# The small-part product of a split fp32r matrix product, taken in bf16

## The chip, the cores and the metric

The kernel runs on one core of one Trainium2 chip. The metric is the device time of one execution in microseconds (us); a run's value is the median of several executions. The core has TensorE (PE in the profile, with its weight loads as PEld), VectorE (DVE), ScalarE (ACT), GpSimd (POOL) and SyncE (SP, which here only issues DMAs). They run side by side and wait for one another through semaphores.

## The reference, cut to what matters

```python
# x (8, 4096, 192), weight_gen (8, 4096, 8, 7), w_in (192, 2048), w_out (2048, 192); all float32 values
w = softmax(weight_gen, axis=-1)                # 7 taps for each row and head
x_unf = the 7 last rows of x, padded with zeros # (B, S, 7, 8 heads, 24)
x = einsum('bshk,bskhg->bshg', w, x_unf).reshape(32768, 192)

h = x @ w_in                                    # the first product, 192 -> 2048
g = h * np.cos(h)
out = g @ w_out                                 # the second product, 2048 -> 192
```

So each row of x is mixed with the six rows before it, the result goes through a product with 2048 columns, each element h becomes h cos h, and a second product brings 2048 back to 192. `w_in` and `w_out` come as float64 words, which the kernel takes apart itself.

## The kernel before, in words

**Batches and periods.** The 32768 rows are worked off in 64 batches of 512 rows (`NB`, 4 rows on each of 128 partitions). The 2048 columns between the two products are taken 256 at a time, as a pair of 128-column chunks, so that a batch has 8 pairs. One pass of the main loop (line 604) handles one pair of one batch; it is called a period below. There are 512 of them, and a few more to drain.

**Split operands.** Both products are made of parts. A value v is cut in v_hi, its fp32r rounding, and v_lo, the rest. The first product is x_lo·w_hi + x_hi·w_lo + x_hi·w_hi, all in fp32r (`ffn_in_first` and `ffn_in_second`, lines 333 to 361). In the second product g_hi meets both parts of `w_out` in one matmul of 384 columns in fp32r, and g_lo, written as bf16, meets a bf16 copy of `w_out` (`wo_b`) in one of 192 columns (`ffn_out`, line 403). So PE already changes between fp32r and bf16 within each period.

**Pairs of matmuls.** The contraction over 192 is cut in three pieces of 64. A matmul of 64 rows uses half of the array; the code issues them two by two, `q` = 0 on partitions 0 to 63 and `q` = 1 on partitions 64 to 127, and the two run side by side. Below, a "pair" of matmuls is such a couple. `wa_hi` and `wa_lo` hold the pieces that meet their own 64 rows of x directly, `wb_hi` and `wb_lo` (half as wide) the middle piece of each chunk. In a period `ffn_in_first` has 3 pairs of 512 columns (line 342) and `ffn_in_second` 6 (line 359); 3 of these 9 have x_lo as the moving operand. `ffn_out` has 8 pairs of 384 and 8 pairs of 192 columns (line 427).

**The order on PE in a period i**: `ffn_in_first(i)`, then `ffn_out(i-6)`: its fp32r half, one pair of small transposes of a later batch's x (line 321), its bf16 half; then `ffn_in_second(i)`. Two periods of every 32 split the bf16 half of `ffn_out` in two and put `ffn_in_first` between them (line 639). All engines work in the order in which the code issues; line 708 onwards pins it.

**The other engines in a period.** ACT turns h into whole turns (line 369), takes the sine (line 383), rounds g to fp32r (line 393), copies the second product's sum out of PSUM every second period (line 450), and rounds the transposed x to x_hi (line 301). DVE takes the fraction (line 379), multiplies (line 386), and writes g_lo as bf16 (line 397). POOL mixes the rows of x with the taps (lines 261 and 276), adds up the outputs (lines 466 and 467), and writes x_lo = x - x_hi (line 303) one 256-column piece at a time. In four batches of the start DVE writes x_lo whole. Once in 32 periods there is a round of softmax for the next 16 rows: ACT loads the table of the exponential, applies it to the taps (line 209) and loads the table of the sine again; in that period DVE makes the turns instead (line 375), and POOL has the sums and scalings of the taps (lines 185 to 188, 217, 206 and 226).

**PSUM.** The tiles `h` take three buffers of two banks, in turn; the sum of the second product (`acc`) takes the last two banks. A period's `h` may be written when DVE is done with the `h` of three periods ago, and `acc` again when ACT has copied it.

**The weights** are cut by `two_parts` (line 124) in steps spread over the first eight periods: ACT makes the size word (134), DVE the bits (136, 140, 144), ACT the fp32r part (147) and, where a `half` is given, a bf16 copy of the whole value (149), POOL the rest (150). Only `w_out` is given a `half` before the change.

The main loop's order around the products, of which the prediction speaks:

```python
if i < N:
    ffn_in_first(i, h_now if whole is None else whole)
if j >= 0:
    ffn_out(j)
...
if i < N:
    ffn_in_second(i)
...
if j >= 0:
    evacuate(j)
```

Of the kernel before, what the change touches and what calls it, by code (L numbers as in the profile page):

```python
# [12 lines left out]
F32R = mybir.dt.float32r  # L13
I32 = mybir.dt.int32
U16 = mybir.dt.uint16
BF16 = mybir.dt.bfloat16
# [4 lines left out]
P = 128  # L21
# [22 lines left out]
def tile_softmax_conv_then_cos_ffn(  # L44
# [14 lines left out]
    F = w_in.shape[1]  # L59
# [4 lines left out]
    CT = R * P  # L64
# [12 lines left out]
    const = ctx.enter_context(tc.tile_pool(name="const", bufs=1))  # L77
    gpool = ctx.enter_context(tc.tile_pool(name="gpool", bufs=9))
    work = ctx.enter_context(tc.tile_pool(name="work", bufs=2))
# [3 lines left out]
    def h_banks(k):  # L83

        return ps_h.tile([P, 2, CT], F32, name="h", tag=f"h{k % 3}", bufs=1)
# [12 lines left out]

    wa_hi = const.tile([P, F], F32R, name="wa_hi")
    wa_lo = const.tile([P, F], F32R, name="wa_lo")  # L100

    wb_hi = const.tile([P, F // 2], F32R, name="wb_hi")
    wb_lo = const.tile([P, F // 2], F32R, name="wb_lo")
    wo = const.tile([P, NFC, 2 * D], F32R, name="wo")
    wo_b = const.tile([P, NFC, D], BF16, name="wo_b")

    def words(n, home="ghi"):

        if home == "ghi":
            raw = gpool.tile([P, 2 * CW], I32, name="raw", tag=home)  # L110
        elif home == "fin":
            raw = work.tile([P, R * D], I32, name="raw", tag=home)
        else:
            raw = work.tile([P, 2 * CT], I32, name="raw", tag=home)
        return raw[:, 0:2 * n]
# [8 lines left out]
    def two_parts(raw, hi, lo, half=None):  # L124
        shape = hi.shape[1:]
        n = math.prod(shape)

        def shaped(t, steps):
            t = t.rearrange("p (n s) -> p n s", s=steps)
            return t if len(shape) == 1 else t.rearrange("p (a b) s -> p a b s", b=shape[1])  # L130

        low, top = (shaped(raw, 2)[..., k] for k in range(2))
        size, bits = (shaped(t[:, 0:n], 1)[..., 0] for t in room.pop(0))
        nc.scalar.activation(out=size.bitcast(F32), in_=top.bitcast(F32), func=AF.Abs, scale=F64_SCALE)
        yield
        nc.vector.tensor_scalar(  # L136
            out=size, in0=size, scalar1=3, scalar2=None, op0=ALU.logical_shift_left)
        yield

        nc.vector.scalar_tensor_tensor(  # L140
            out=size, in0=top, scalar=-0x80000000, in1=size, op0=ALU.bitwise_and, op1=ALU.bitwise_or)
        yield

        nc.vector.scalar_tensor_tensor(  # L144
            out=bits, in0=low, scalar=29, in1=size, op0=ALU.logical_shift_right, op1=ALU.bitwise_or)
        yield
        nc.scalar.copy(out=hi, in_=bits.bitcast(F32))
        if half is not None:
            nc.scalar.copy(out=half, in_=bits.bitcast(F32))
        nc.gpsimd.tensor_tensor(out=lo, in0=bits.bitcast(F32), in1=hi.bitcast(F32), op=ALU.subtract)  # L150

    def w_in_a(c0, c1, home="ghi"):
        raw = words(c1 - c0, home)
        for n in range(2):
            nc.sync.dma_start(out=raw[n * D2:(n + 1) * D2],
                              in_=w_in[n * P:n * P + D2, c0:c1].bitcast(I32))
        return two_parts(raw, wa_hi[:, c0:c1], wa_lo[:, c0:c1])

    w_in_odd_even = w_in.rearrange("k (a n c) -> n k a c", n=2, c=P)

    def w_in_b(j):
        raw = words(CW)
        pairs = slice(j * CW // P, (j + 1) * CW // P)
        for n in range(2):
            nc.sync.dma_start(out=raw[n * D2:(n + 1) * D2].rearrange("k (a c) -> k a c", c=2 * P),
                              in_=w_in_odd_even[1 - n, D2:P, pairs, :].bitcast(I32))
        cols = slice(j * CW, (j + 1) * CW)
        return two_parts(raw, wb_hi[:, cols], wb_lo[:, cols])

    w_out_v = w_out.rearrange("(c p) d -> p c d", p=P)  # L170

# [113 lines left out]
    def traded(t):  # L285

        nc.sync.keepalive_nop([nc.sync.lower_ap(t)])
# [4 lines left out]
    def parts_of(b):  # L292
        if b not in xT:
            hi = work.tile([P, 2, CT], F32R, name="x_hi")
            lo = work.tile([P, 2, CT], F32R, name="x_lo")
            xT[b] = (hi, lo)
        return xT[b]

    def split(b, t, cs, eng):
        hi, lo = parts_of(b)  # L300
        nc.scalar.copy(out=hi[:, :, cs], in_=t)
        yield
        eng.tensor_tensor(
            out=lo[:, :, cs], in0=t, in1=hi[:, :, cs].bitcast(F32), op=ALU.subtract)
# [25 lines left out]
    def chunk(pair, n):  # L330
        return slice((2 * pair + n) * P, (2 * pair + n + 1) * P)

    def ffn_in_first(i, h=None):

        b, pair = divmod(i, NPAIR)
        x_hi, x_lo = xT[b]
        if h is None:
            h = h_banks(i)
        for m, (w, v) in enumerate(((wa_hi, x_lo), (wa_lo, x_hi), (wa_hi, x_hi))):
            for q in range(2):  # L340
                rs = slice(q * D2, (q + 1) * D2)
                nc.tensor.matmul(  # L342
                    h[:, q, :], lhsT=w[rs, chunk(pair, q)], rhs=v[rs, q, :],
                    start=(m == 0), stop=False, skip_group_check=True)
        hs[i] = h
        traded(h)

    def ffn_in_second(i):

        b, pair = divmod(i, NPAIR)  # L350
        x_hi, x_lo = xT[b]
        h = hs[i]
        prods = ((wa_hi, x_lo, 0), (wa_lo, x_hi, 0), (wb_hi, x_lo, 1), (wb_lo, x_hi, 1),
                 (wa_hi, x_hi, 0), (wb_hi, x_hi, 1))
        for m, (w, v, middle) in enumerate(prods):
            for q in range(2):
                rs = slice(q * D2, (q + 1) * D2)
                cs = slice(pair * P, (pair + 1) * P) if middle else chunk(pair, 1 - q)
                nc.tensor.matmul(  # L359
                    h[:, 1 - q, :], lhsT=w[rs, cs], rhs=v[rs, q ^ middle, :],  # L360
                    start=False, stop=(m == len(prods) - 1), skip_group_check=True)
# [163 lines left out]
    def all_of(*steps):  # L525
# [4 lines left out]

    late = [
        (-1, 1, w_in_a, (768, 1280)), (-1, 2, w_in_b, (1,)), (-1, 2, w_out_2, (0,)),
        (0, 3, w_in_a, (1280, 1792)), (0, 3, w_out_2, (1,)), (1, 4, w_out_2, (2, "part1")),
        (1, 4, w_out_2, (3, "part1")), (2, 5, w_in_a, (1792, 2048, "fin")),
        (2, 5, w_out_2, (4, "fin")), (4, 6, w_out_2, (5, "part1")), (4, 7, w_out_2, (6, "part1")),
        (5, 8, w_out_2, (7, "fin")),
# [19 lines left out]
    next(sm1)  # L556
    w_a0 = w_in_a(0, 256)
    w_b0 = w_in_b(0)
    load_rows(1)
    w_a1 = w_in_a(256, 768)  # L560
# [43 lines left out]
    for i in range(N + LAG + 1):  # L604
# [23 lines left out]
        def products():  # L628
            if b < NB and pair == 0:
                assert b in transposed  # L630
            if whole is not None and j >= 0:

                ffn_out(j)
                ffn_in_first(i, whole)
            elif j >= N - HALF:
                if j == N - HALF:
                    last_half()
                return
            elif busy and EXP + 2 <= step <= EXP + 3:

                ffn_out(j, rest=False)
                ffn_in_first(i)
                ffn_out(j, rest=True)
            else:
# [6 lines that stand above are left out]
            if j in stores:  # L651
                stores.pop(j)()
            if j >= 0:
                evacuate(j)
# [91 lines left out]
```

## Time and profile before

| what | value |
|---|---|
| median of 3 runs | 2257.45 us (2256.27 to 2257.81) |
| span of the profiled execution, first to last instruction | 2256.1 us |
| PE busy, matmuls | 2203.8 us, 98% of the span, 26496 matmuls |
| PE busy, weight loads (beside the matmuls) | 2009.9 us, 89% |
| DVE, ACT, POOL busy | 1922.0 (85%), 1886.0 (84%), 2001.4 (89%) us |
| mean granted clock of TensorE | 0.993 |
| DMA queue, share of its 16 engines | 18.4% |

The profile is of one execution. Its rows carry the line of the code, the engine, the operation, out<-in by the program's names, partitions x elements and type, a count and times. fp32r operands of matmuls are shown as f32. A matmul's duration holds its run through the array, so that matmuls overlap one another in the rows and the pace of the stream is read from starts, not from durations. "idle before, releaser" is the time that an engine stood still and what ended it. Windows are stretches in us from the start of the span.

### The profile page before, as it was taken

The numbers are of one execution on the slowest core, as the hardware profiler recorded it, in microseconds if no ns is written. First come the engines' busy times: TensorE is split into PE (matmuls) and PEld (weight loads), VectorE is DVE, ScalarE is ACT, GpSimd is POOL, SyncE is SP. The second block draws the span as 40 slices with busy tenths as digits, with TensorE's granted clock in tenths as the row PEclk, the third lists the DMA queues.
The fourth block names the chain that finished last, engine by engine and source line by source line (L and its number), as shares of the span: only waits on it lengthen the run. The fifth ranks groups of instructions, "written<-read, shape, count | busy, mean of one in ns | idle before, by whom it ended". The sixth has DMA issues, their size and how long they took to land.

```text
span 2256.1 us, 60616 instructions
## 1 busy us (share of the span) xinstructions
PE 2203.8 (98%) x26496; PEld 2009.9 (89%) x26496; DVE 1922.0 (85%) x1663; ACT 1886.0 (84%) x2111; POOL 2001.4 (89%) x1460
## 2 busy tenths in 40 slices
PE   4899999999999999999999999999999999999998
PEld 2788889889999889999999988899999999899887
DVE  7888888888888888888888888888888888888887
ACT  4788888888888888888888888888888888888886
POOL 7999999998998989989998998989989899899941
PEclk8899999999999999999999999999999999999999
DMA  6221121121221221221211211211211211212100
GB/s 157 57 59 43 33 59 39 46 51 34 51 50 36 49 59 26 50 59 27 58 46 31 59 44 41 51 43 42 51 48 37 58 30 47 59 26 53 33 9 22
DMA packets 25767, 105.55 MB, mean 47 GB/s; under 512 B 2734, under 2 KB 6566, under 8 KB 25502
## 3 DMA queue, kind: packets, MB, share of 16 engines
q1 hardware_dynamic: 25502, 101.67, 18.4%
q8 instruction: 208, 3.41, 0.6%
q14 instruction: 57, 0.47, 0.1%
HBM read 76.50 MB, written 25.17 MB: 45 GB/s over the span
## 4 chain that ended last, share of the span: by engine, by line
PE 94%; DVE 2%; ACT 2%; POOL 1%; issue 1%; DMA 0%; SPq 0%; POOLq 0%; DVEq 0%; ACTq 0%
PE acc L427 45%; PE h L359 31%; PE h L342 16%; PE acc L321 1%; DVE glo L397 1%; ACT part L450 1%; ACT ghi L393 1%; POOL xa L276 1%; POOL pr L261 1%; PE h L491 0%; DVE turn L379 0%; DMA xt<-in_x_dram 0%; DVE h L140 0%; DVE h L136 0%; PE h L312 0%
## 5 line engine op out<-in xcount | busy, mean ns | idle before, releaser
L379 DVE TENSOR_TENSOR turn<-h,turn 128x1024 f32<-128x1024 f32 x512 | 625.5, 1222 | 281.2 <-ACT turn L369 281.2
L427 PE MATMUL acc<-wo,ghi 64*128 64x384 f32 x8112 | 807.2, 335 | 0.3 <-ACT part L454 0.3
L427 PEld LDWEIGHTS acc<-wo,ghi 64*128 64x128 f32 x8112 | 736.7, 185 | 35.9 <-ACT part L450 3.1
L276 POOL TENSOR_TENSOR xa<-xa,pr 128x768 f32<-128x768 f32 (+1 forms) x384 | 703.0, 1831 | 0.6
L383 ACT ACTIVATE turn<-turn 128x1024 f32<-128x1024 f32 x512 | 543.4, 1061 | 188.5 <-DVE turn L379 185.1
L386 DVE SCALAR_TENSOR_TENSOR h<-h,turn 128x1024 f32<-128x1024 f32 x512 | 631.0, 1233 | 20.3 <-ACT turn L383 20.3
L397 DVE TENSOR_TENSOR glo<-h,ghi 128x1024 bf16<-128x1024 f32 x512 | 622.5, 1216 | 2.7 <-ACT ghi L393 1.7
L369 ACT ACTIVATE turn<-h 128x1024 int32<-128x1024 f32 x497 | 510.2, 1027 | 125.5 <-PE h L359 118.6
L261 POOL TENSOR_TENSOR pr<-xt,taps 128x768 f32<-128x768 f32 (+1 forms) x384 | 589.5, 1536 | 11.9
L393 ACT CAST ghi<-h 128x1024 fp32r<-128x1024 f32 x512 | 518.0, 1012 | 14.2 <-DVE h L386 14.2
L427 PE MATMUL acc<-wo_b,glo 64*128 64x192 bf16 x8112 | 431.1, 243 | 0.0
L466 POOL TENSOR_TENSOR part<-part,part 128x768 f32<-128x768 f32 x126 | 234.3, 1859 | 157.2 <-ACT part L450 130.3
L427 PEld LDWEIGHTS <-glo 64*128 64x128 bf16 x8112 | 333.5, 94 | 23.0 <-issue 11.0
L359 PE MATMUL h<-x_lo,wa_hi 64*128 64x512 f32 x1024 | 253.0, 477 | 0.7
L450 ACT COPY part<-acc 128x1024 f32<-128x1024 f32 x240 | 239.6, 998 | 3.6 <-PE acc L427 3.6
L342 PE MATMUL h<-x_lo,wa_hi 64*128 64x512 f32 x1024 | 217.3, 407 | 20.5 <-DVE t L144 14.1
L359 PE MATMUL h<-x_lo,wb_hi 64*128 64x512 f32 x1024 | 211.8, 397 | 0.0
L342 PE MATMUL h<-x_hi,wa_lo 64*128 64x512 f32 x1024 | 210.1, 392 | 1.3 <-POOL wa_lo L150 1.3
L359 PE MATMUL h<-x_hi,wa_hi 64*128 64x512 f32 x1024 | 211.1, 395 | 0.0
L342 PE MATMUL h<-x_hi,wa_hi 64*128 64x512 f32 x1024 | 210.5, 393 | 0.0
L359 PE MATMUL h<-x_hi,wb_hi 64*128 64x512 f32 x1024 | 208.6, 390 | 0.0
L359 PE MATMUL h<-x_hi,wb_lo 64*128 64x512 f32 x1024 | 208.5, 390 | 0.0
(73 smaller groups left out, 2163.3 us busy)
## 6 DMA issues: line engine op xcount, KB each, us to landing
xt<-in_x_dram SPq DMA_DIRECT2D x62, 960.0 KB, 6.8
out_dram<-fin SPq DMA_DIRECT2D x63, 384.0 KB, 3.4
taps<-in_weight_gen_dram SPq DMA_DIRECT2D x15, 448.0 KB, 4.8
raw<-in_moe_w_out_dram SPq DMA_DIRECT2D x8, 384.0 KB, 4.2
raw<-in_moe_w_in_dram SPq DMA_DIRECT2D x10, 256.0 KB, 10.8
xt<-in_x_dram SPq DMA_DIRECT2D x1, 768.0 KB, 10.5
xt<-in_x_dram SPq DMA_DIRECT2D x1, 540.0 KB, 5.5
raw<-in_moe_w_in_dram SPq DMA_DIRECT2D x4, 128.0 KB, 4.6
```

The costliest lines, as they stand in the source:

```text
L261: eng.tensor_tensor(out=dst.rearrange("p r (h g) -> p r h g", h=H), in0=xt[:, k + ra:k + rb, :].rearrange("p r (h g) -> p r h g", h=H), in ...
L276: eng.tensor_tensor(out=acc if k < K else xa, in0=acc, in1=old[:, ra:rb], op=ALU.add)
L342: nc.tensor.matmul(h[:, q, :], lhsT=w[rs, chunk(pair, q)], rhs=v[rs, q, :], start=(m == 0), stop=False, skip_group_check=True)
L359: nc.tensor.matmul(h[:, 1 - q, :], lhsT=w[rs, cs], rhs=v[rs, q ^ middle, :], start=False, stop=(m == len(prods) - 1), skip_group_check=True)
L369: nc.scalar.activation(out=t.bitcast(I32), in_=hs[i], func=AF.Identity, bias=0.25, scale=1.0)
L379: nc.vector.tensor_tensor(out=t, in0=hs[i], in1=t.bitcast(I32), op=ALU.subtract)
L383: nc.scalar.activation(out=t, in_=t, func=AF.Sin, bias=SIN_BIAS, scale=SIN_SCALE)
L386: nc.vector.scalar_tensor_tensor(out=hs[i], in0=hs[i], scalar=TWO_PI, in1=turns.pop(i), op0=ALU.mult, op1=ALU.mult)
L393: nc.scalar.copy(out=hi, in_=hs[i])
L397: nc.vector.tensor_tensor(out=lo, in0=hs.pop(i), in1=hi.bitcast(F32), op=ALU.subtract)
L427: nc.tensor.matmul(to, lhsT=g[rs, n, t * P:(t + 1) * P], rhs=w[rs, fc, :], start=(lo == 0 and c == 0 and (whole or s == 0)), stop=(lo == 1 ...
L450: nc.scalar.copy(out=part, in_=acc)
```

## The change

`w_in` gets bf16 copies, `wa_b` and `wb_b`, made by the `half` step that `two_parts` already has (seven more ACT copies, one for each piece of `w_in`). x_lo becomes a bf16 tile. The three pairs of a period that move x_lo take `wa_b`, `wb_b` as weights instead of `wa_hi`, `wb_hi`; both operands are then bf16. In `ffn_in_second` the two x_lo pairs are put ahead of the two w_lo pairs, where they alternated before. The six pairs that move x_hi stay fp32r. The number of matmuls, their sizes and the sums in PSUM are the same.

```diff
     wa_lo = const.tile([P, F], F32R, name="wa_lo")
+    wa_b = const.tile([P, F], BF16, name="wa_b")
...
     wb_lo = const.tile([P, F // 2], F32R, name="wb_lo")
+    wb_b = const.tile([P, F // 2], BF16, name="wb_b")
...
-        return two_parts(raw, wa_hi[:, c0:c1], wa_lo[:, c0:c1])
+        return two_parts(raw, wa_hi[:, c0:c1], wa_lo[:, c0:c1], wa_b[:, c0:c1])
...
-        return two_parts(raw, wb_hi[:, cols], wb_lo[:, cols])
+        return two_parts(raw, wb_hi[:, cols], wb_lo[:, cols], wb_b[:, cols])
...
-            lo = work.tile([P, 2, CT], F32R, name="x_lo")
+            lo = work.tile([P, 2, CT], BF16, name="x_lo")
...
-        for m, (w, v) in enumerate(((wa_hi, x_lo), (wa_lo, x_hi), (wa_hi, x_hi))):
+        for m, (w, v) in enumerate(((wa_b, x_lo), (wa_lo, x_hi), (wa_hi, x_hi))):
...
-        prods = ((wa_hi, x_lo, 0), (wa_lo, x_hi, 0), (wb_hi, x_lo, 1), (wb_lo, x_hi, 1),
+        prods = ((wa_b, x_lo, 0), (wb_b, x_lo, 1), (wa_lo, x_hi, 0), (wb_lo, x_hi, 1),
                  (wa_hi, x_hi, 0), (wb_hi, x_hi, 1))
```

PE in the middle of the program, one period from the end of the bf16 half of `ffn_out` to the next period's fp32r half, before (an "x2" is a pair; a bf16 matmul has its LDWEIGHTS as an instruction of its own, an fp32r matmul loads its weights itself):

```order
L427 LDWEIGHTS glo
L427 MATMUL acc<-wo_b,glo 128x192
L359 MATMUL h<-x_lo,wa_hi 128x512 x2
L359 MATMUL h<-x_hi,wa_lo 128x512 x2
L359 MATMUL h<-x_lo,wb_hi 128x512 x2
L359 MATMUL h<-x_hi,wb_lo 128x512 x2
L359 MATMUL h<-x_hi,wa_hi 128x512 x2
L359 MATMUL h<-x_hi,wb_hi 128x512 x2
L342 MATMUL h<-x_lo,wa_hi 128x512 x2
L342 MATMUL h<-x_hi,wa_lo 128x512 x2
L342 MATMUL h<-x_hi,wa_hi 128x512 x2
L427 MATMUL acc<-wo,ghi 128x384 x16
```

The same place on PE after the change, whose lines stand two lower (359 is 361, 342 is 344, 427 is 429); each bf16 pair is two LDWEIGHTS and two MATMULs, of which one couple is shown:

```order
L429 LDWEIGHTS glo
L429 MATMUL acc<-wo_b,glo 128x192
L361 LDWEIGHTS wa_b
L361 MATMUL h<-x_lo,wa_b 128x512
L361 LDWEIGHTS wb_b
L361 MATMUL h<-x_lo,wb_b 128x512
L361 MATMUL h<-x_hi,wa_lo 128x512 x2
L361 MATMUL h<-x_hi,wb_lo 128x512 x2
L361 MATMUL h<-x_hi,wa_hi 128x512 x2
L361 MATMUL h<-x_hi,wb_hi 128x512 x2
L344 LDWEIGHTS wa_b
L344 MATMUL h<-x_lo,wa_b 128x512
```

Two x_lo pairs now stand right behind the bf16 half of `ffn_out`, and the third stands alone between fp32r pairs: a period changes from fp32r to bf16 and back twice instead of once.

ACT at the start of the program, after the change, at the first three pieces of `w_in` (t is the piece's bits):

```order
L303 CAST x_hi<-h 128x1024
L149 CAST wa_hi<-t_175 128x256
L151 CAST wa_b<-t_175 128x256
L149 CAST wb_hi<-t_175 128x512
L151 CAST wb_b<-t_175 128x512
L136 ACTIVATE h<-raw 128x512
L149 CAST wa_hi<-t_211 128x512
L151 CAST wa_b<-t_211 128x512
```

The rows of line 151 are new; what followed on ACT now stands behind them. DVE, POOL and SP keep their order.

## The prediction

> **What bounds the kernel now.** I read the page first, then stretches, then PE's instructions in order of time. From the page, the span, PE and the chain that ended last:
>
> ```profile
> span 2256.1 us, 60616 instructions
> PE 94%; DVE 2%; ACT 2%; POOL 1%; issue 1%; DMA 0%; SPq 0%; POOLq 0%; DVEq 0%; ACTq 0%
> ```
>
> PE is 94% of the chain. Two stretches of the windows, the second up to the last pair of the first product (length, then busy us of PE, PEld, DVE, ACT, POOL):
>
> ```profile
> 120.00:158.00 38.00, 37.91 (x452) 33.66 (x450) 31.77 (x28) 30.44 (x33) 36.64 (x23) 1.00 0.18 42
> 158.00:2236.90 2078.90, 2076.60 (x25315) 1905.59 (x25311) 1784.06 (x1508) 1776.63 (x1976) 1860.90 (x1351) 1.00 0.18 44
> ```
>
> From 120 us on PE is without a hole (37.91 of 38.00, 2076.60 of 2078.90), at the full granted clock (1.00); DVE and ACT are busy 86% and 85%, POOL 90%. So a shorter PE period is worth its time until another engine becomes late. PE's timeline over one ordinary period (start, length, idle in brackets if any):
>
> ```profile
> 1020.37 0.39 PE L359 MATMUL h<-x_hi,wa_lo 64*128 64x512 f32 x2
> 1020.59 0.41 PE L359 MATMUL h<-x_lo,wb_hi 64*128 64x512 f32 x2
> ...
> 1021.53 0.41 PE L342 MATMUL h<-x_lo,wa_hi 64*128 64x512 f32 x2
> ...
> 1022.23 1.58 PE L427 MATMUL acc<-wo,ghi 64*128 64x384 f32 x16
> 1023.63 0.23 PE L321 MATMUL acc<-ident,xa 64*128 64x64 f32 x2
> 1023.69 0.83 PE L427 MATMUL acc<-wo_b,glo 64*128 64x192 bf16 x16
> ...
> 1024.61 0.40 PE L359 MATMUL h<-x_hi,wa_lo 64*128 64x512 f32 x2
> ```
>
> From 1020.37 to 1024.61 is one period, 4.24 us. From 1020.37 to 1022.23 stand eight fp32r pairs of 512 columns: 1.86 / 8 = 0.2325 us each. From 1022.23 to 1023.63, eight fp32r pairs of 384: 0.175 each. The matmuls' own lengths (0.4) overlap and are no pace.
>
> **The change part by part.**
>
> *The pace of a bf16 pair.* The trace has no bf16 pair of 512 columns; the nearest is that of 192. In one of the two periods per 32 where the bf16 half is cut in two, PE runs:
>
> ```profile
> 1014.25 0.51 PE L427 MATMUL acc<-wo_b,glo 64*128 64x192 bf16 x8
> 1014.53 0.49 PE L342 MATMUL h<-x_lo,wa_hi 64*128 64x512 f32 x2
> 1014.84 0.41 PE L342 MATMUL h<-x_hi,wa_lo 64*128 64x512 f32 x2
> 1015.07 0.41 PE L342 MATMUL h<-x_hi,wa_hi 64*128 64x512 f32 x2
> 1015.31 0.52 PE L427 MATMUL acc<-wo_b,glo 64*128 64x192 bf16 x8
> ```
>
> Eight matmuls take 0.51, sixteen (above) 0.83: four more pairs in 0.32, 0.080 each; with the rounding of the rows 0.078 to 0.083. In proportion to columns, 512 cost 0.208 to 0.220; if a few ns of a pair don't grow with the columns, a little less. I take 0.217, near the upper end, so 0.0155 saved for each of three pairs, 0.0465 us a period (bounds 0.0125 and 0.0245 a pair).
>
> *Entering fp32r from bf16.* From 1014.25 to 1014.84 is 0.59, and holds four bf16 pairs (0.32) and the x_lo pair (0.2325): 0.03 to 0.04 too much. The weight loads say why. From the page, the loads of `ffn_out`, fp32r and bf16 (busy us, mean ns); then PEld's timeline at the same place:
>
> ```profile
> L427 PEld LDWEIGHTS acc<-wo,ghi 64*128 64x128 f32 x8112 | 736.7, 185 | 35.9 <-ACT part L450 3.1
> L427 PEld LDWEIGHTS <-glo 64*128 64x128 bf16 x8112 | 333.5, 94 | 23.0 <-issue 11.0
> ```
>
> ```profile
> 1014.50 0.21 PEld L342 LDWEIGHTS h<-x_lo,wa_hi 64*128 64x128 f32 x2
> 1014.61 0.21 PEld L342 LDWEIGHTS h<-x_hi,wa_lo 64*128 64x128 f32 x2
> 1014.85 0.20 PEld L342 LDWEIGHTS h<-x_hi,wa_hi 64*128 64x128 f32 x2
> 1015.31 0.29 PEld L427 LDWEIGHTS <-glo 64*128 64x128 bf16 x8 [0.26 <-issue]
> ```
>
> A load starts when the matmul before it starts (1014.85 beside the matmul of 1014.84). The fp32r load of x_lo's weights starts at 1014.50 with the last bf16 pair; the next pair's load, which starts with x_lo's matmul, is at 1014.61. So the stream waited 0.11 us for an fp32r load, and only 0.08 of bf16 work covered it: 0.03 stuck out. After the change the fp32r load stands behind a bf16 pair of 0.217, which covers 0.11 twice. So in `ffn_in_second` 0.03 goes, and the lone bf16 pair of `ffn_in_first` does not bring it back. The Trainium skill, "TensorE: Matmul & The Clock Gate", section "LDWEIGHTS (loading the stationary operand)", has a load take its columns over 1.2, so an estimate of 107 ns for 128 columns whatever the rows; the 0.11 agrees, and by it too the 0.03 is a load that sticks out, not a price of changing type.
>
> *Entering bf16 from fp32r.* Here a load is not early: at 1015.31 it starts with its matmul, [0.26] after the last, though the fp32r pair started at 1015.07. The pace is 0.24 instead of 0.2325, and the eight matmuls behind it take 0.52, not 0.51: 0.018 us. In `ffn_in_second` the bf16 block already exists and only grows; in `ffn_in_first` a new one begins behind fp32r: +0.018.
>
> A period gains 0.0465 + 0.03 - 0.018 = 0.0585 us. The same order of pairs stays on PE, and no wait is added there.
>
> *What is late next.* Once in 32 periods ACT switches tables for the taps, and POOL has their sums. There the rows are, in order of time, of ACT, POOL and PE, and last POOL's busy time in the stretch from its first to its last row here:
>
> ```profile
> 999.83 1.03 ACT L369 ACTIVATE turn<-h 128x1024 int32<-128x1024 f32 x1
> 1001.78 1.28 ACT L209 ACT_TABLE_LOAD   x1
> 1006.31 0.39 ACT L301 CAST x_hi<-part 128x256 fp32r<-128x256 f32 x1
> 1006.77 0.74 POOL L303 TENSOR_TENSOR x_lo<-part,x_hi 128x256 fp32r<-128x256 f32 x1 [0.88 <-ACT x_hi L301]
> 1041.77 0.73 POOL L303 TENSOR_TENSOR x_lo<-part,x_hi 128x256 fp32r<-128x256 f32 x1
> 1042.75 0.40 PE L342 MATMUL h<-x_lo,wa_hi 64*128 64x512 f32 x2
> 1006.77:1042.50 35.73, 35.01 (x29) 1.00 0.20 49
> ```
>
> ACT's run of table loads, exponential and sine ends in x_hi at 1006.31, POOL starts on it and then never waits (35.01 of 35.73 busy, the rest 29 small gaps); its last piece of the next batch's x_lo ends at 1042.50, and PE's first pair that reads it starts at 1042.75. So PE has at most 0.25 us in hand; I take 0.2. ACT's run starts with the turns of 999.83, as soon as PE has made that h; from there to 1042.75 lie 42.9 / 4.24 = 10 periods. Ten periods faster by 0.0585 bring PE there 0.585 early: 0.385 is lost again, waiting for POOL. How often: the row of DVE's turns, which only those rounds have, counts 15, and the last round is a short one of four rows:
>
> ```profile
> DVE turn L375 <- PE h L359: 12.4, 15, 0.8
> ```
>
> 14 x 0.385 = 5.4 us lost, and some 0.2 for the short one. Elsewhere POOL, at 90%, goes to 91%, ACT and DVE to 87%: nobody is late.
>
> *x_lo as bf16 on POOL.* The trace has no bf16 written by POOL's tensor_tensor. The nearest rows: POOL with fp32r and with f32 output of 384 columns, and DVE with bf16 and f32 output:
>
> ```profile
> L150 POOL TENSOR_TENSOR wo<-t,wo 128x384 fp32r<-128x384 f32 x8 | 8.0, 1004 | 2.1 <-ACT wo L147 2.1
> L467 POOL TENSOR_TENSOR fin<-part 128x384 f32<-128x384 f32 x126 | 127.6, 1013 | 9.9
> L397 DVE TENSOR_TENSOR glo<-h,ghi 128x1024 bf16<-128x1024 f32 x512 | 622.5, 1216 | 2.7 <-ACT ghi L393 1.7
> L379 DVE TENSOR_TENSOR turn<-h,turn 128x1024 f32<-128x1024 f32 x512 | 625.5, 1222 | 281.2 <-ACT turn L369 281.2
> ```
>
> The output's type costs neither engine anything (1004 against 1013, 1216 against 1222), so I take 0, with -0.1 to +0.1 us a piece as own range. The stretch above holds five such pieces, so 0.1 each is 0.5 x 14 = 7 us more, or at most the 5.4 back.
>
> *The seven copies on ACT.* The casts that stand there give their price, and a sine later in the start phase its cover:
>
> ```profile
> L147 ACT CAST wa_hi<-t 128x512 fp32r<-128x512 f32 x3 | 1.8, 612 | 3.1 <-DVE t L144 3.1
> L147 ACT CAST wa_hi<-t 128x256 fp32r<-128x256 f32 x2 | 0.8, 398 | 0.0
> 44.91 1.06 ACT L383 ACTIVATE turn<-turn 128x1024 f32<-128x1024 f32 x1 [2.68 <-DVE turn L379]
> ```
>
> Five of 0.61 and two of 0.40: 3.9 us of ACT. From the second period on they lie in ACT's idle time ahead of such sines (2.68 here). The first three (0.40 + 0.61 + 0.61) stand ahead of the first turns: between 0 and 1.6 us, I take 0.5. Without that cover all 3.9 would count.
>
> **The sum.** From 120 us on, where PE's holes end, to 2236.9 lie 2116.9 / 4.24 = 499 periods, some three less since those of the table rounds are longer: 496. 496 x 0.0585 = 29.0; less 5.4, 0.2 and 0.5: 22.9 us. Span 2256.1 - 22.9 = 2233.2; the median of the runs is 1.35 above this execution's span, so 2234.5. The forecast's own range: at best three pairs at 0.0245, entry into fp32r 0.03 and 0.01 of entry into bf16 give 0.0935 a period, 46 less 14 x 0.735 and 0.5: 35, so 2222; at worst 0.0375 + 0.03 - 0.03 gives 18.6, less 2.4, less 1.6, and 3 for POOL: 11, so 2246.
>
> **The rivals.**
>
> 1. *The 0.03 is a price of changing type.* Then `ffn_in_second` keeps it and `ffn_in_first` pays it anew: 0.0465 - 0.018 - 0.03 = 0, and with the copies 2258, no change. For it: every bf16 to fp32r entry in the trace has a short pair ahead, so it can't be told apart by size. Against it: the 0.11 between the two loads. 0.14, with mixtures from 2248 to 2259.
>
> 2. *Slower: POOL's x_lo.* If writing bf16 costs POOL e us more a piece, a stretch of ten periods grows by 5e - 0.2 over today. Outside, 356 periods gain 20.8. It turns slower from 14 x (5e - 0.2) = 20.8, e = 0.34, half as long again as 0.74. At double length it gives 14 x 3.5 = 49 less 20.8: 28 slower, 2285. POOL's 240 pieces would then fill 178 us more, 98% of the stretch. Against it: the four rows. 0.06.
>
> 3. *Each bf16 load waits for its own half of the array.* Loads of 94 ns at three pairs a period would stick out whole: 0.28 - 0.0465 - 0.03 = +0.2, 100 us slower, 2358. Against it: eight bf16 loads of 94 take 0.29 beside eight matmuls of 0.52, so they run under them. That is the rule of the Trainium skill, same page, Part 3, "The mechanism": loads overlap running matmuls only where the row group differs. The bf16 rows contradict it; the load at 1015.31 alone looks like it, at 0.018. 0.02.
>
> **How the numbers follow.** Forecast 0.75; rival 1 0.14; rival 2 0.06; rival 3 0.02; 0.03 for a gain past 2222. The range 2222 to 2256 holds the forecast but for its edges (0.72) and most of rival 1 (0.09): 0.81. A measurement of this kernel tells about 0.2%, 4.5 us, from no change. Faster: 0.75 + 0.03 and a small part of rival 1, 0.80; same: the rest of it, 0.11; slower: rivals 2 and 3 and a bad edge, 0.09.
>
> **What would show it.** In the profile after: the period from one x_hi,wa_lo pair of `ffn_in_second` to the next near 4.18 us; bf16 pairs of 512 paced at 0.217; the x_lo pairs behind `ffn_out` with nothing sticking out; the load of the lone pair's weights late, that of the fp32r pair behind it early; a new wait of PE for POOL's x_lo in 14 batches of about 0.4 us; x_lo on POOL still near 740 ns. I am wrong if the lone bf16 pair takes 0.25 or more with the pair behind it late, if x_lo on POOL passes 1 us, or if the waits for POOL eat most of the gain.

## The result

| | median | runs | profiled span |
|---|---|---|---|
| before | 2257.02 us | 2256.27 to 2257.81 (4) | 2256.1 us |
| after | 2230.37 us | 2230.04 to 2230.68 (4) | 2228.2 us |

The ratio is 0.988, with a 95% interval of 0.9866 to 0.9894: 26.7 us or 1.2% less. The forecast was 2234.5 us. From the page of after, the span and the engines on the chain that ended last:

```profile
span 2228.2 us, 60412 instructions
PE 65%; POOL 22%; ACT 6%; DVE 4%; issue 3%; DMA 0%; SPq 0%; POOLq 0%; ACTq 0%; DVEq 0%
```

PE had 94% of the chain before and has 65% now; POOL has 22%, where it had 1%. The long stretch of the windows (length, then busy us of PE, PEld, DVE, ACT, POOL):

```profile
158.00:2208.90 2050.90, 2044.36 (x25302) 1764.65 (x25298) 1781.72 (x1507) 1761.94 (x1974) 1859.24 (x1350) 1.00 0.18 44
```

The stretch is 28.0 us shorter, and PE now stands still 6.5 us in it instead of 2.3. (A matmul's row holds its run through the array, so short waits of PE don't show here.) PE's timeline of after over one ordinary period, which begins in the last pairs of `ffn_out`'s bf16 half:

```profile
985.69 0.82 PE L429 MATMUL acc<-wo_b,glo 64*128 64x192 bf16 x16
986.35 0.38 PE L361 MATMUL h<-x_lo,wa_b 64*128 64x512 bf16 x2
986.57 0.38 PE L361 MATMUL h<-x_lo,wb_b 64*128 64x512 bf16 x2
986.59 0.58 PE L361 MATMUL h<-x_hi,wa_lo 64*128 64x512 f32 x2
987.01 0.39 PE L361 MATMUL h<-x_hi,wb_lo 64*128 64x512 f32 x2
987.24 0.40 PE L361 MATMUL h<-x_hi,wa_hi 64*128 64x512 f32 x2
987.47 0.40 PE L361 MATMUL h<-x_hi,wb_hi 64*128 64x512 f32 x2
987.71 0.39 PE L344 MATMUL h<-x_lo,wa_b 64*128 64x512 bf16 x2
987.75 0.58 PE L344 MATMUL h<-x_hi,wa_lo 64*128 64x512 f32 x2
988.17 0.39 PE L344 MATMUL h<-x_hi,wa_hi 64*128 64x512 f32 x2
988.40 1.57 PE L429 MATMUL acc<-wo,ghi 64*128 64x384 f32 x16
...
990.52 0.38 PE L361 MATMUL h<-x_lo,wa_b 64*128 64x512 bf16 x2
```

From 986.35 to 990.52 is one period, 4.17 us; it was 4.24. From 985.69 to 986.35 lie the eight bf16 pairs of 192, 0.66, and nothing sticks out behind them. A bf16 pair of 512 goes on after 0.22 (986.35 to 986.57; 0.216 over all). From 986.57 to 987.01, 0.44, lie the second bf16 pair and the fp32r pair behind it: 0.216 and 0.22 to 0.23 (0.231 over all periods), no more than the 0.2327 of an fp32r pair among its own before the change, so entering fp32r is free here. From 987.47 to 987.71, the entry into the lone bf16 pair, is 0.24. (The early start and the length of the rows at 986.59 and 987.75 are taken up in the last section.)

The pace over 14 periods without a softmax round (first to last start of a period's last pair; each period has two such matmuls, so x30 is 15 periods), of before and then of after:

```profile
L359 PE MATMUL h<-x_hi,wb_hi x30: 388/388/401, 1046.8 to 1106.2; 64*128 64x512 f32 x30
```

```profile
L361 PE MATMUL h<-x_hi,wb_hi x30: 393/393/398, 1034.5 to 1093.0; 64*128 64x512 f32 x30
```

That is 59.4 / 14 = 4.243 and 58.5 / 14 = 4.179. Averaged from the ends of each period's last pair, over all stretches without a round, the ordinary period went from 4.246 to 4.1735, 0.073 us less. Below, periods, the parts of a period and their means are worked out from such ends, so they stand in no row as they are. The same over 14 periods with a round in them, of before and of after:

```profile
L359 PE MATMUL h<-x_hi,wb_hi x30: 387/388/401, 999.4 to 1059.5; 64*128 64x512 f32 x30
```

```profile
L361 PE MATMUL h<-x_hi,wb_hi x30: 387/393/398, 987.5 to 1047.1; 64*128 64x512 f32 x30
```

Here 60.1 became 59.6: of 14 x 0.073 = 1.02 us only half arrives.

### The profile page after: what moved, and what is told of

It reads as the page before. It is cut to its first block, busy times and chain, and to the rows that moved or that the text cites. A ratio compares the mean times of both kernels' runs of the same rounds, so it can differ in the third digit from the quotient of the medians.

```text
span 2228.2 us, 60412 instructions
## 1 busy us (share of the span) xinstructions
PE 2169.7 (97%) x26496; PEld 1862.0 (84%) x26496; DVE 1921.8 (86%) x1663; ACT 1875.4 (84%) x2118; POOL 2000.8 (90%) x1460
## 4 chain that ended last, share of the span: by engine, by line
PE 65%; POOL 22%; ACT 6%; DVE 4%; issue 3%; DMA 0%; SPq 0%; POOLq 0%; ACTq 0%; DVEq 0%
PE acc L429 32%; PE h L361 21%; PE h L344 11%; POOL xa L278 7%; POOL pr L263 5%; POOL part L468 2%; POOL x_lo L305 2%; DVE turn L381 1%; POOL fin L469 1%; ACT turn L371 1%; POOL taps L228 1%; ACT turn L385 1%; POOL xa L263 1%; POOL den L190 1%; ACT L385 1%
## 5 line engine op out<-in xcount | busy, mean ns | idle before, releaser
L344 PE MATMUL h<-x_hi,wa_lo 64*128 64x512 f32 x1024 | 305.4, 581 | 1.7 <-POOL wa_lo L152 1.7
L361 PE MATMUL h<-x_hi,wa_lo 64*128 64x512 f32 x1024 | 305.9, 582 | 0.0
L344 PE MATMUL h<-x_lo,wa_b 64*128 64x512 bf16 x1024 | 207.3, 389 | 25.0 <-DVE t L146 13.4
L305 POOL TENSOR_TENSOR x_lo<-part,x_hi 128x256 bf16<-128x256 f32 x240 | 177.2, 741 | 28.9 <-ACT x_hi L303 28.9
```

The lines of the kernel that those rows point to most:

```text
L344: nc.tensor.matmul(h[:, q, :], lhsT=w[rs, chunk(pair, q)], rhs=v[rs, q, :], start=(m == 0), stop=False, skip_group_check=True)
L361: nc.tensor.matmul(h[:, 1 - q, :], lhsT=w[rs, cs], rhs=v[rs, q ^ middle, :], start=False, stop=(m == len(prods) - 1), skip_group_check=True)
```

## The experiments

Theory A is the prediction's: what sticks out at a change of type is a weight load that the work before it does not cover, and the rest of the gain is the pace of bf16. Rival 1 gives each change of type a price of its own. The second question is where half of the gain around a round goes.

**e1: bf16 and fp32r pairs alternate in the second group.**

```diff
-        prods = ((wa_b, x_lo, 0), (wb_b, x_lo, 1), (wa_lo, x_hi, 0), (wb_lo, x_hi, 1),
+        prods = ((wa_b, x_lo, 0), (wa_lo, x_hi, 0), (wb_b, x_lo, 1), (wb_lo, x_hi, 1),
```

> The changed kernel, but in the second group of the first product the bf16 and fp32r pairs alternate (x_lo by wa, x_hi by wa_lo, x_lo by wb, x_hi by wb_lo), as before the change. A period then enters bf16 three times instead of twice. Theory A (what sticks out at a change of type is the weight load that the work before it doesn't cover): entering fp32r behind a bf16 pair of 512 columns is free, entering bf16 costs 0.017 us, so an ordinary period goes from 4.173 to 4.190, some 340 periods outside the stretches that POOL sets pay it: 5.8 us, 2236. Rival 1 (a change of type has a price of its own of 0.03 when entering fp32r): 0.047 a period, 16 us, 2246.

Measured: 2232.57 us, ratio to before 0.9889 (0.9874 to 0.9905). The 14 periods behind a round in e1:

```profile
L361 PE MATMUL h<-x_hi,wb_hi x30: 393/393/393, 1035.5 to 1094.1; 64*128 64x512 f32 x30
```

58.6 / 14 = 4.186, and 4.182 over all such stretches: less than the 4.190 of theory A and far from the 4.22 of rival 1. The third entry into bf16 costs its 0.017 (a bf16 pair behind fp32r takes 0.2325, one behind bf16 0.216). The fp32r pairs behind those of the second group take 0.228 each: no 0.03 sticks out at any of them, and rival 1 falls. The times alone don't separate this kernel from the changed one, as their intervals overlap.

**e8: the lone pair of the first group as fp32r again** (with x_hi in the place of x_lo):

```diff
-        for m, (w, v) in enumerate(((wa_b, x_lo), (wa_lo, x_hi), (wa_hi, x_hi))):
+        for m, (w, v) in enumerate(((wa_hi, x_hi), (wa_lo, x_hi), (wa_hi, x_hi))):
```

> The changed kernel, but the lone pair of the first group is an fp32r pair again; for lack of an fp32r x_lo it moves x_hi with wa_hi, so that product is computed twice there and x_lo's share on its own 64 rows is left out. Theory A: a lone bf16 pair between fp32r pairs gains 0.017 in its pace and 0.004 behind it and pays 0.017 at its entry, so the period goes from 4.173 to no more than 4.18; as x_lo is needed only in the second group, the wait for POOL (14 x 0.28) goes: 2228. Rival: each of the three pairs bears a third of the gain, 0.0245; 4.198, and 8 less 4 us slower: 2235. If a type change had a price of its own of 0.03, the lone pair would be a loss, and this kernel would be faster: 2215.

Measured: 2226.70 us, ratio 0.9862 (0.9846 to 0.9879). Its 14 periods behind a round:

```profile
L361 PE MATMUL h<-x_hi,wb_hi x30: 387/388/388, 1033.1 to 1091.6; 64*128 64x512 f32 x30
```

58.5, as in after; the ordinary period is 4.174 here and 4.1735 in after. So the lone bf16 pair is worth nothing, as its entry costs what its pace gains. The whole gain of the change sits in the two pairs behind `ffn_out`. The kernel is faster than after by 3.7 us; the period in which the first group of after waits for x_lo (e9, below) is an ordinary one here, which is worth 14 x 0.29 = 4.1 us.

**e3 and e4: before and after without the exponential of the loop's rounds.**

```diff
-        nc.scalar.activation(out=t, in_=t, func=AF.Exp)
+        if early:
+            nc.scalar.activation(out=t, in_=t, func=AF.Exp)
```

> The kernel before, leaving out the exponential of the taps in the softmax rounds of the main loop, and with it ACT's two table loads in each round. Only to be compared with the same cut in the changed kernel. The rounds' periods should fall from 4.68, 4.28 and 4.45 us to near 4.25; 15 x 0.6 = 9 us: 2248.

> The changed kernel with the same cut. Theory A says that what the change gains in ordinary periods (0.0735 us) is lost in a stretch of 11 periods behind each round because ACT's run of table loads and exponential holds POOL and PE there. Without that run nothing is lost: the gain between the two cut kernels is 496 x 0.0735 = 36 us (2248 to 2212), against 26.7 between the whole ones. Rival: POOL is late by its work alone, or the gain is less elsewhere; then the two cut kernels differ by 27 as well.

Measured: 2257.07 us (ratio to before 0.9999, 0.999 to 1.0009) and 2225.64 us (0.9859, 0.9841 to 0.9877). The difference is 31.4, between the two expectations, and e3's own expectation of 2248 failed: without the exponential and its table loads the round's three long periods stayed at 4.68, 4.28 and 4.45 us. The waits of e3 (total, times, longest) show what ACT and DVE wait for then:

```profile
ACT part L451 <- PE acc L428: 50.9, 15, 3.4
DVE glo L398 <- ACT ghi L394: 19.5, 15, 1.3
```

In the round's order ACT must copy the sum before it rounds g; without the exponential it stands 3.4 us waiting for that sum, and DVE's g_lo waits behind it, so that the h buffer comes no earlier. In e4 the period eight behind the round, 4.467 on average in after, is 4.177: ACT's x_hi, and POOL with it, start earlier without ACT's run, and PE finds x_lo ready. That wait and no other goes here, and the rounds keep their length, which is why the gain lies between the two.

**e6 and e7: the same cut, and the ordinary order in the rounds.**

```diff
-        exps = busy and step == EXP
+        exps = False
...
-        early_sums = busy and step == EXP + 1
+        early_sums = False
...
-            elif busy and EXP + 2 <= step <= EXP + 3:
+            elif False:
```

(The two other conditions on `EXP` go in the same way.)

> The kernel before as in e3 (the exponential of the loop's rounds left out), and the order that the code takes in those rounds (turns on DVE, the products ahead of the fp32r copy, the bf16 half cut in two) replaced by the ordinary one. e3 has shown that the rounds' long periods stay without the exponential. Theory: that order, which lets DVE make the turns behind PE, sets them; now all periods are near 4.25 and 15 x 0.65 = 10 us go: 2247. Rival: POOL's and DVE's work of the softmax itself sets them; 2257.

> The changed kernel with the same cut and order as e6. Theory: without the rounds' order and ACT's run every one of 496 periods gains the 0.0735 us of an ordinary one, 36 us under e6, 2211. Rival: POOL or DVE are late by their work alone at this pace; then the gain stays near the 31 us between e4 and e3.

Measured: 2247.62 us (0.9957, 0.9943 to 0.9972) and 2214.30 us (0.9809, 0.9794 to 0.9823). In e6 the ordinary periods and the rounds' alike are 4.247, as expected. Between e6 and e7 lie 33.3 us, of the 36 expected. In e7 the round's three periods are ordinary; what is left is the period eight behind it, 4.354 (14 x 0.18), and the one four before it, 4.257 (15 x 0.084). In the first of these PE's x_lo pair starts 0.05 us behind the end of POOL's x_lo in all 14 batches, so the rival is right in part: once the round's periods are ordinary and PE comes there 0.9 us earlier than in e4, POOL is late without ACT's run too. So the rounds cost 2257.0 - 2247.6 = 9.4 us before the change and 2230.4 - 2214.3 = 16.1 after it. The 6.7 us between the two are gain of the change that the rounds take back.

**e9: the lone pair last in its group.**

```diff
-        for m, (w, v) in enumerate(((wa_b, x_lo), (wa_lo, x_hi), (wa_hi, x_hi))):
+        for m, (w, v) in enumerate(((wa_lo, x_hi), (wa_hi, x_hi), (wa_b, x_lo))):
```

> The changed kernel, with the lone bf16 pair as the last of the three pairs of the first group instead of the first. The entry into bf16 and the covered load behind it stay, so ordinary periods stay at 4.173. x_lo is needed two pairs, 0.46 us, later. If PE's long period in every fourth batch (4.46) is the wait for POOL's x_lo at that pair, it falls to 4.18: 14 x 0.28 = 4 us, 2226.5. If that period is long for another reason (the h buffer, DVE), nothing changes: 2230.5.

Measured: 2231.55 us, ratio 0.9889 (0.9871 to 0.9907). First the place in after, PE and POOL, in the period eight behind a round:

```profile
1029.82 0.75 POOL L305 TENSOR_TENSOR x_lo<-part,x_hi 128x256 bf16<-128x256 f32 x1
1030.11 0.41 PE L361 MATMUL h<-x_hi,wb_hi 64*128 64x512 f32 x2
1030.62 0.39 PE L344 MATMUL h<-x_lo,wa_b 64*128 64x512 bf16 x2
```

PE goes on 0.51 behind the pair at 1030.11 instead of 0.24, 0.05 after POOL's x_lo ends at 1030.57. It is 0.05 in all 14 such batches of after; before the change it was 0.22 to 0.26 in all but the first. The same place in e9:

```profile
1030.47 0.75 POOL L305 TENSOR_TENSOR x_lo<-part,x_hi 128x256 bf16<-128x256 f32 x1
1030.88 0.39 PE L361 MATMUL h<-x_hi,wb_hi 64*128 64x512 f32 x2
1031.11 0.40 PE L344 MATMUL h<-x_hi,wa_lo 64*128 64x512 f32 x2
1031.58 0.39 PE L344 MATMUL h<-x_lo,wa_b 64*128 64x512 bf16 x2
```

PE passes x_lo's end at 1031.22 without a stop, and the long period falls from 4.467 to 4.176. That settles the wait for POOL's x_lo. But the time did not fall: the ordinary periods of e9 average 4.182, 0.0085 more than after's, which over some 430 of them is 3.6 us, nearly the 14 x 0.29 that the wait gave. And the start is 1.5 us longer: the 21st period ends at 140.6 us, in after at 139.1. The 0.0085 lies in the two fp32r pairs of the first group, which take 0.2335 each here and 0.229 in after, where they stand behind the lone bf16 pair; why both of them do, and why the start is longer, stays open.

**e2, e5, e10: the lone pair beside the bf16 half of `ffn_out`.**

```diff
+            if lo == 0 and between is not None:
+                ffn_in_lo(between)      # the pair (wa_b, x_lo) of the first group
...
-                if i < N:
-                    ffn_in_first(i, h_now if whole is None else whole)
+                apart = i < N and j >= 0                # so in e2
+                apart = i < N and j >= 0 and j % 2 == 0 # so in e5
+                apart = i < N and j >= 0 and j % 2 == 1 # so in e10, with the order of e9
+                if i < N:
+                    ffn_in_first(i, h_now if whole is None else whole, lo=not apart)
...
-                    ffn_out(j)
+                    ffn_out(j, between=i if apart else None)
```

> The changed kernel, but the lone x_lo pair of the first group is taken out from between the fp32r pairs and put right ahead of the bf16 half of the second product, so that all bf16 work of a period is one block. Theory A: an ordinary period loses the 0.017 us of the second entry into bf16, 4.173 to 4.156; x_lo is needed 2 us later, so PE's wait for POOL's x_lo in every fourth batch (about 0.28 us, 14 times) goes: 430 x 0.017 + 14 x 0.28 = 11 us, 2219. Rival 1 (a price of the type change on both sides): 0.047 a period and the wait, 24 us, 2206. If the wait for POOL is no real limit but only how the chain is drawn, 7 us: 2223.

> As e2, but the x_lo pair is moved beside the bf16 half only in the periods behind which the sum is not copied out (every second one). In e2 PE waited 240 times for ACT's copy of the sum, 52 us in all, because the moved pair shortened the time between the sum's end and its next use; these periods keep the order of the changed kernel here. Theory A: every second period saves the second entry into bf16, 0.013 to 0.017 us, 215 times: 3 us; the first period of a batch is among them, so the wait for POOL's x_lo in every fourth batch, 14 x 0.28, goes as well: 2223. If the wait for POOL only moves to another place: 2227.

> As e9, and in the other half of the periods than in e5, those whose sum is copied out, the lone pair stands beside the bf16 half of the second product. In e5 the pair was taken from the period behind the copy, so that PE still came to the sum's banks too early (49.6 us of waits, as in e2); here the three pairs stay between the sum's end and its next use. Every second period should save the second entry into bf16, 0.013 to 0.017 us: 3 us under e9, 2223.5. If ACT's copy is late anyway, no gain over e9.

Measured: e2 2230.31 (0.9879, 0.9863 to 0.9895), e5 2232.82 (0.9891, 0.9876 to 0.9906), e10 2226.93 (0.9867, 0.9852 to 0.9883). PEld's waits for ACT's copy of the sum in after, e2, e5 and e10:

```profile
PEld acc L429 <- ACT part L452: 12.7, 45, 0.4
```

```profile
PEld acc L440 <- ACT part L465: 52.2, 240, 0.5
```

```profile
PEld acc L440 <- ACT part L465: 49.6, 240, 0.5
```

```profile
PEld acc L440 <- ACT part L465: 2.8, 15, 0.2
```

In e2 the moved pair, 0.216 us, is taken out of the time between the sum's end and the next write to its banks, which was 1.88 us in after, and ACT's copy ended only 0.36 ahead. The fp32r load for that write is due a pair, 0.23, before it. So the copy is now late for the load every time there is one, 240 times. The wait for x_lo is gone (4.176), but an ordinary period keeps only 0.005 of the 0.017 on average, and where ACT and DVE are behind, PE pays for the copy in full: the round's three periods grow by 0.22 us and the one four before it by 0.20. 430 x 0.005 + 14 x 0.29 - 15 x 0.42 = 0, as measured.

e5 was to leave the periods alone whose sum is copied, but it took the pair from the first group that stands between the sum's end and its next use: my choice of the half was wrong, and the wait stayed, with the same 0.2 us in the same places. e10 takes the other half: the wait is gone, the round is as in after, ordinary periods are 4.168 and the one eight behind the round 4.172. At 2226.93 us it is the fastest of the versions that compute the whole reference, 3.4 us under the changed kernel. The runs of the two don't overlap (2226.61 to 2227.31 against 2230.04 to 2230.68), though the intervals of their ratios do. By its periods it should have gained 6: its 21st period ends at 142.0 us, after's at 139.1, and why the start is longer was not looked into.

## Why the prediction was right, point by point

**The pace of a bf16 pair** was taken at 0.217 and is 0.216; against 0.2327, the mean of the eight fp32r pairs of before that don't stand behind bf16, that is 0.0168 a pair, 0.050 a period (forecast 0.0465).

**Entering fp32r.** The pair that paid it took 0.2603 before the change, so 0.028 stuck out. That is gone, and the lone pair does not bring it back. PEld's timeline of after:

```profile
990.74 0.19 PEld L361 LDWEIGHTS h<-x_hi,wa_lo 64*128 64x128 f32 x2
990.96 0.19 PEld L361 LDWEIGHTS h<-x_hi,wb_lo 64*128 64x128 f32 x2
...
991.89 0.10 PEld L344 LDWEIGHTS <-wa_b 64*128 64x128 bf16 x2 [0.28 <-issue]
991.89 0.20 PEld L344 LDWEIGHTS h<-x_hi,wa_lo 64*128 64x128 f32 x2
992.12 0.19 PEld L344 LDWEIGHTS h<-x_hi,wa_hi 64*128 64x128 f32 x2
```

The fp32r loads start with the bf16 matmul ahead of them (990.74, and 991.89 beside the lone pair), and the next load follows 0.22 to 0.23 later: the bf16 pair's own time, and no more. That it is the cover that counts, and not where the pair stands, is seen in e10: in one period of each round an fp32r pair of the first group stands behind a short bf16 pair of 192 again. PEld and PE there:

```profile
1002.68 0.19 PEld L344 LDWEIGHTS h<-x_hi,wa_lo 64*128 64x128 f32 x2
1002.79 0.19 PEld L344 LDWEIGHTS h<-x_hi,wa_hi 64*128 64x128 f32 x2
```

```profile
1002.44 0.49 PE L440 MATMUL acc<-wo_b,glo 64*128 64x192 bf16 x8
1002.71 0.48 PE L344 MATMUL h<-x_hi,wa_lo 64*128 64x512 f32 x2
1003.02 0.40 PE L344 MATMUL h<-x_hi,wa_hi 64*128 64x512 f32 x2
```

The two loads lie 0.11 apart as in the prediction's rows, and the fp32r pair takes 0.259 (over 13 rounds): the same change of type, 0.03 dearer behind 0.08 of work than behind 0.216. (It is not the change from the sum's banks to h's either: the bf16 pair behind `ffn_out` makes it in after at 0.216.) The 0.11 is read from the distance of loads alone; the loads' own rows are longer (0.19).

A size was off on the good side: the six fp32r pairs of a period, which as six of before's would take 6 x 0.2327 = 1.396, take 1.3865, 0.010 less. Where that comes from stays open; after's ordinary periods also alternate, 4.181 and 4.166, mostly in these pairs, and e8's do not.

**Entering bf16** costs 0.016 (0.2323 against 0.2159; forecast 0.018): the lone pair's load comes late, [0.28], as the row shows. Together 0.050 + 0.028 + 0.010 - 0.016 = 0.072 of the 0.073 measured (the rest is in `ffn_out`), where 0.0585 was forecast. So the gain of a period was taken 0.0145 too small, mostly for the 0.010 that had no term: 496 x 0.0145 = 7.2 us. Against it the losses of the next point were taken 3.4 too small. That the two errors partly cancel is luck. They leave 3.8 of the 5.0 us between the forecast span, 2233.2, and the measured 2228.2.

**What is late next** was right in its mechanism for the main part: PE waits for POOL's x_lo in every fourth batch, 14 times 0.29 us (forecast 0.385). The 0.2 in hand was right too: from ACT's turns to PE's x_lo pair lay 42.9 us before, and lie 42.7 after (987.92 to 1030.62). But I put the whole loss there and had nobody late elsewhere, and the runs show three places. The round's own three periods sum to 13.41 us before and 13.43 after, whatever PE's pace: 15 x 0.24 = 3.6 us of gain lost, in the order of the round and not in the table loads (e3, e6). The wait for POOL takes 14 x 0.29 = 4.1. The period four before a round went from 4.252 to 4.262 while its neighbours fell, 15 x 0.084 = 1.3. One such place in after, DVE, ACT and PEld:

```profile
1110.52 1.08 DVE L206 TENSOR_REDUCE top<-taps 128x128 f32<-128x896 f32 x1
1112.76 1.06 ACT L385 ACTIVATE turn<-turn 128x1024 f32<-128x1024 f32 x1 [0.69 <-DVE turn L381]
1113.72 1.00 ACT L452 COPY part<-acc 128x1024 f32<-128x1024 f32 x1
1114.77 1.35 PEld L429 LDWEIGHTS acc<-wo,ghi 64*128 64x128 f32 x16 [0.26 <-ACT part L452]
```

DVE takes the maximum of the taps there, ACT's sine waits 0.69 for DVE where it waits 0.39 in the periods beside it, its copy of the sum ends at 1114.72, and the load of `ffn_out` waits for that copy. No run took this chain away by itself. That is 9.0 us lost, 5.6 forecast. The account then closes to 0.7: 496 x 0.073 - 9.0 = 27.2, and the span fell by 27.9.

**x_lo as bf16 on POOL.** The rows of before and of after:

```profile
L303 POOL TENSOR_TENSOR x_lo<-part,x_hi 128x256 fp32r<-128x256 f32 x240 | 177.1, 741 | 30.5 <-ACT x_hi L301 30.3
L305 POOL TENSOR_TENSOR x_lo<-part,x_hi 128x256 bf16<-128x256 f32 x240 | 177.2, 741 | 28.9 <-ACT x_hi L303 28.9
```

741 ns before and after: rival 2 had no ground. Rival 3 falls by the pace of the bf16 pairs.

**The copies on ACT** were priced at 0.5 us of the start; the 21st period of the program ends at 139.1 us, at 140.4 before, with the first gains of the loop in it (20 x 0.073 = 1.5), so next to no loss is seen.

## What to carry to other kernels

Where a matmul's type changes, ask which weight load stands at the border and what runs above it: putting the two cheaper pairs next to work of their own type gave all of the gain, and the third, alone between pairs of the other type, gave nothing. A gain on the engine that sets the pace is worth its full size only in the stretches where it does; find the stretches that another engine's chain spans, and count the periods in them out. And before moving work, look at which time it is taken out of: a pair that cost nothing where it stood was the cover of ACT's copy.

## What the runs showed of the hardware that I had not expected

The loads behave differently in the two directions. An fp32r load starts with the matmul ahead of it, whichever type that has (990.74 above beside a bf16 pair; 1014.85 in the prediction beside an fp32r pair). The bf16 load of the lone pair, behind an fp32r product, did not: it started 0.235 us after that pair's start, together with its own matmul (991.89, [0.28]), in all 393 ordinary periods of after; the 0.016 is what then sticks out. Behind the small fp32 transposes ahead of `ffn_out`'s bf16 half it is not late: there the load starts with the transposes (both at 989.81). And the row of an fp32r matmul right behind a bf16 pair begins 0.02 to 0.04 us after that pair's row (986.59 and 987.75 above) and lasts 0.58 us on average, as here in after's page, though these pairs are paced at 0.229 to 0.231: such a row's start and length are no times of work.

```profile
L361 PE MATMUL h<-x_hi,wa_lo 64*128 64x512 f32 x1024 | 305.9, 582 | 0.0
```
